# New placing numbers for every step of a one-core attention and MLP kernel

## The chip, the core and the metric

The kernel runs on one core of a Trainium2 chip. The metric is the time of one execution on the device in microseconds (us); the time before is the median of three runs. The engines have the profile's names: PE is TensorE (PEld its weight load), DVE is VectorE, ACT is ScalarE, POOL is GpSimd, SP is SyncE, whose queue issues most DMAs.

## What is computed

The reference is an attention in clusters, followed by a mixing of rows and an MLP:

```python
q_n = q / (norm(q) + 1e-06); k_n, c_n likewise          # q, k, v: (4, 8, 768, 64)
q_assign = argmax(einsum('bhsd,hcd->bhsc', q_n, c_n), axis=-1)   # 16 clusters for each head
k_assign = argmax(einsum('bhsd,hcd->bhsc', k_n, c_n), axis=-1)
scores = where(q_assign[..., :, None] == k_assign[..., None, :], q @ k^T / 8, -1e9)
attn = exp(scores - max(scores)); attn = attn / (sum(attn) + 1e-09)
x = attn @ v                                             # (4, 768, 512) with the heads side by side
h = x^T @ U @ V                                          # U: 768x32, V: 32x768
u = x + h^T
out = u + relu(u @ w1) @ w2                              # w1: 512x2048, w2: 2048x512
```

U, V, w1 and w2 come as 64-bit floats. The kernel takes them as 32-bit words and joins each pair of words to one 32-bit float by itself.

## The kernel before, in words

**The work.** The attention has 16 tasks, one for each batch and pair of heads, of 12 slots each (NS). A task loads queries and keys (L343) and values (L349), finds each row's cluster (`sims` L353, `largest`, `clusters`, `clusters_T` L389), splits queries and keys into a coarse and a fine part (`split_hi` L400 on ACT, `split_lo` L404 on POOL or DVE), and copies the parts and the one-hot clusters by DMA on SP to their places in a large tile named `arena` (`place_keys_hi`, `place_keys_lo`, `place_queries`, `place_ones`, `place_clusters`, all through L237). Then come the row maxima (`rowmax`, PE at L467, DVE at L469), their transpose and placing (`rowmax_T`, `rowmax_place`), the scores (PE at L505 and L507) with the exponential on ACT (L510), the running sum of the exponentials in T (`weights`, L520, on POOL with ten exceptions on DVE), the product with v (L528) and the division by the sum. After the four tasks of a batch the rows are mixed with U and V (`mix_u`, `mix_sum`, `mix_v`).

**The MLP.** It has 32 groups (g0 to g31), each a slice of 256 of the 2048 hidden columns for the 768 rows of a batch: four slices of batch 0, all eight of batch 1, the other four of batch 0, then batches 2 and 3. A group's first product is done in seven smaller products (`product` L726, PE at L735 to L737) of sums of the weights' quarters (`add_w`, POOL at L701) with sums of u's quarters (`add_u`, POOL at L679). All factors are split into a coarse part (ACT at L685, L710, L719) and a fine part by a subtraction of two SBUF tiles: L686 for u on DVE, L708 for the first weights on POOL up to group 12 and on DVE after that, L717 for the second weights on POOL. Each product's PSUM tile `ps_h`, of which there are two, is taken up by a combine on DVE (L745; the first product's by ACT at L749). A relu on ACT (L778) and its fine part on DVE (L775) follow, then the second product (`gemm2`, PE at L788 to L790). At the end of a run of groups `finish` adds the result to u (DVE at L798).

**The weights.** The 32 halves of the weights' blocks are joined from words by `load_weights` (12 halves, during the attention) and `convert` (20 halves, during the first MLP groups): a load (L624), a scaling on ACT (L626), three operations on DVE in `merge` (a shift L194, an and/or L195, a shift/or L197) and a store. In `load_weights` L194 writes to PSUM; in `convert` all three work on SBUF tiles. While the last attention task runs, u of the first batch is turned and split (`turn_u`, `splits`); the later batches are turned two groups ahead of their own first group, in groups 2, 14 and 22, and the splits of their sums stand in those groups and in the next.

**The order.** Nothing is ordered by a scheduler. Each step is put in a plan with a time (`at`, L810); the plan is sorted by time and written out, and `keep_order` (L133) ties each engine's instructions in that order. The times come from tables at L58 to L130, in slots of the attention (12 for a task) and, after it, units of which a group has seven, one for each product:

- `times`: for every step of an attention task, one column for each of six kinds of tasks (most; last of a batch; last; first; second; third). `lead`, `paces` and `spots` set the scores of task 0 and the places of the row maxima.
- `order0`: the order of the steps of `start`, which opens the program.
- `mixes`, `stages`, `PACE`: the row mixing and the stages of the weights' joining; `joins` gives the base time of each of the 20 halves of `convert`.
- `mlp`: the steps of the groups. `split0` places the splits of u for the first batch, `split` those for the later ones, `add_w`, `split_w`, `split_w2`, `relu` and `gemm2` the rest; `first` and `second` hold the times of groups 0 and 1.

An engine that waits for one step holds back all that stands behind it in its order, whatever that needs.

## Time and profile before

| | before |
|---|---|
| median of 3 runs | 1030.05 us (1029.45 to 1030.70) |
| profiled execution | 1033.91 us |
| its span in the trace | 1032.1 us |
| mean granted PE clock | 0.987 |
| PE busy | 979.0 us |
| DVE, ACT, POOL busy | 715.4, 443.1, 622.8 us |
| attention (about) | 0 to 475 us |
| groups of the MLP | about 475 to 1032 us |

The page gives busy time and share by engine, and a row of digits for the granted clock of PE in 40 slices (9 is 90% or more). The list of waits gives engine and line, what it waited for, and total, times and longest in us. In a timeline a row has its start, its duration, the engine, the line, and out<-in by the program's names; brackets give the idle time ahead of it and what ended it. The view by stretches gives for each the start and end, the length, busy time of each engine with the number of its instructions, PE's granted clock, the share of DMA and its rate.

### The profile page before, as it was taken

The numbers are of one execution on the slowest core, as the hardware profiler recorded it, in microseconds if no ns is written. First come the engines' busy times: TensorE is split into PE (matmuls) and PEld (weight loads), VectorE is DVE, ScalarE is ACT, GpSimd is POOL, SyncE is SP. The second block draws the span as 40 slices with busy tenths as digits, with TensorE's granted clock in tenths as the row PEclk, the third lists the DMA queues.
The fourth block names the chain that finished last, engine by engine and source line by source line (L and its number), as shares of the span: only waits on it lengthen the run. The fifth ranks groups of instructions, "written<-read, shape, count | busy, mean of one in ns | idle before, by whom it ended". The sixth has DMA issues, their size and how long they took to land.

```text
span 1032.1 us, 14214 instructions
## 1 busy us (share of the span) xinstructions
PE 979.0 (95%) x5227; PEld 764.5 (74%) x5227; DVE 715.4 (69%) x1110; ACT 443.1 (43%) x633; POOL 622.8 (60%) x420
## 2 busy tenths in 40 slices
PE   7999999999999999989978999899989999899998
PEld 4666665666666666655966978788878988788887
DVE  5798877777777777486589678756585545865453
ACT  4454554565555544663433424232433224432320
POOL 5476675787777867995578465754454444644320
PEclk8999999999999999999998999999999999999999
DMA  7665565565556647002534643436223222241221
GB/s 176 180 146 151 144 169 172 151 183 149 150 186 157 184 118 235 21 1 72 194 104 174 208 158 123 153 115 221 111 70 116 83 102 91 93 143 42 82 82 62
DMA packets 42505, 135.99 MB, mean 132 GB/s; under 512 B 6410, under 2 KB 11012, under 8 KB 41924
## 3 DMA queue, kind: packets, MB, share of 16 engines
q1 hardware_dynamic: 42064, 135.00, 42.8%
q8 instruction: 41, 0.67, 0.3%
q14 instruction: 28, 0.23, 0.1%
q10 hardware_dynamic: 372, 0.10, 0.0%
HBM read 81.26 MB, written 22.54 MB: 101 GB/s over the span
## 4 chain that ended last, share of the span: by engine, by line
PE 72%; DVE 19%; issue 3%; ACT 3%; DMA 1%; POOL 1%; ACTq 0%; SPq 0%; DVEq 0%; POOLq 0%
PE o_ps L528 11%; PE ps_max L467 7%; PE y L789 7%; PE y L790 7%; PE y L788 7%; PE ps_h L735 6%; PE ps_h L736 6%; PE ps_h L737 6%; PE st L505 5%; PE st L507 5%; DVE m L469 2%; DVE hl L775 2%; DVE combos L708 2%; DVE arena L686 2%; DVE c L745 1%
## 5 line engine op out<-in xcount | busy, mean ns | idle before, releaser
L469 DVE TENSOR_REDUCE m<-ps_max 128x1 f32<-128x384 f32 x384 | 194.2, 549 | 84.7 <-PE ps_max L467 82.7
L520 POOL TENSOR_TENSOR T<-T,pr 128x768 f32<-128x768 f32 x120 | 226.2, 1885 | 40.6 <-ACT pr L510 16.7
L510 ACT ACTIVATE pr<-st 128x768 f32<-128x768 f32 x192 | 154.7, 812 | 78.8 <-PE st L507 66.1
L778 ACT ACTIVATE hh<-c 128x768 fp32r<-128x768 f32 x64 | 54.2, 847 | 285.6 <-DVE c L745 285.6
L735 PE MATMUL ps_h<-arena,combos 128*128 128x384 f32 x384 | 133.0, 346 | 22.4 <-DVE rw_g L745 11.7
L789 PE MATMUL y<-w,hh 128*128 128x512 f32 x384 | 153.3, 399 | 0.0
L788 PE MATMUL y<-w,hh 128*128 128x512 f32 x384 | 152.7, 398 | 0.0
L790 PE MATMUL y<-w,hl 128*128 128x512 f32 x384 | 152.2, 396 | 0.0
L467 PE MATMUL ps_max<-arena 128*128 128x384 f32 x384 | 124.0, 379 | 9.3 <-ACT ohT L394 2.0
L528 PE MATMUL o_ps<-pr,vt 128*64 128x384 f32 x768 | 131.6, 491 | 0.1
L736 PE MATMUL ps_h<-arena,combos 128*128 128x384 f32 x384 | 130.5, 340 | 0.0
L737 PE MATMUL ps_h<-arena,combos 128*128 128x384 f32 x384 | 130.1, 339 | 0.0
L505 PE MATMUL st<-arena 128*128 128x384 f32 x384 | 104.2, 353 | 3.0 <-ACT pr L510 3.0
L467 PEld LDWEIGHTS ps_max<-arena 128*128 128x128 f32 x384 | 69.0, 191 | 49.2 <-DVE m L469 14.0
L520 POOL TENSOR_TENSOR T<-pr 128x768 f32<-128x768 f32 x30 | 56.9, 1898 | 79.8 <-ACT pr L510 79.8
L775 DVE SCALAR_TENSOR_TENSOR hl<-c,hh 128x768 fp32r<-128x768 f32 x64 | 80.9, 1264 | 30.9 <-ACT hh L778 30.9
L735 PEld LDWEIGHTS ps_h<-arena,combos 128*128 128x128 f32 x384 | 72.8, 190 | 39.3 <-DVE rw_g L745 13.4
L507 PE MATMUL st<-arena 97*128 97x384 f32 x384 | 99.8, 341 | 1.6 <-DMA arena<-mT 1.6
L528 PEld LDWEIGHTS o_ps<-pr,vt 128*64 128x64 f32 x768 | 52.0, 137 | 66.2 <-issue 60.7
L701 POOL TENSOR_TENSOR sums_w<-rw 128x256 f32<-128x256 f32 x64 | 58.9, 939 | 50.2 <-DVE combos L708 50.2
L717 POOL TENSOR_TENSOR w<-w2f,w 128x1024 fp32r<-128x1024 f32 x16 | 39.7, 2479 | 80.3 <-ACT w L719 80.3
L790 PEld LDWEIGHTS y<-w,hl 128*128 128x128 f32 x384 | 72.7, 189 | 16.6
(143 smaller groups left out, 1708.0 us busy)
## 6 DMA issues: line engine op xcount, KB each, us to landing
rw<-w_scr SPq DMA_DIRECT2D x30, 512.0 KB
u<-u_scr SPq DMA_DIRECT2D x18, 768.0 KB
R<-in_qk SPq DMA_DIRECT2D x32, 384.0 KB
arena<-arena SPq DMA_DIRECT2D x32, 384.0 KB
arena<-arena SPq DMA_DIRECT2D x64, 192.0 KB
late_rw<-in_w SPq DMA_DIRECT2D x20, 512.0 KB
w2f<-w_scr SPq DMA_DIRECT2D x14, 512.0 KB
w2f_odd<-w_scr SPq DMA_DIRECT2D x14, 512.0 KB
```

What stands on the lines that cost most here:

```text
L467: nc.tensor.matmul(ps[:, 0:HS], x1[:, 0, g // 2, g % 2, t * P:(t + 1) * P], x1[:, 1, h, g % 2, :], start=True, stop=True)
L469: nc.vector.reduce_max(live["m2", i][:, h, u:u + 1], ps[:, 0:HS], axis=AX.X)
L505: nc.tensor.matmul(st[:, j, 0:HS], x1[:, 1, hk, j, ks], x1[:, 0, h, j, :], start=True, stop=False)
L510: nc.scalar.activation(pr, st[:, :, 0:HS], AF.Exp, scale=SCALE)
L520: eng.tensor_add(T, live["p", i, h, 0] if c == 1 else T, live["p", i, h, c])
L528: nc.tensor.matmul(o_ps[64 * j:64 * j + 64, 0:HS], vv[:, c, j, :], pr[:, j, :], start=(c == 0), stop=(c == NT - 1))
L735: nc.tensor.matmul(ps, ah[:, d], oh[:, d], start=(d == 0), stop=False)
L736: nc.tensor.matmul(ps, ah[:, d], ol[:, d], start=False, stop=False)
L737: nc.tensor.matmul(ps, al[:, d], oh[:, d], start=False, stop=(d == 1))
L788: nc.tensor.matmul(y, hh[:, f, ts], w2[:, 0, f, :], start=(g in firsts and f == 0), stop=False)
L789: nc.tensor.matmul(y, hh[:, f, ts], w2[:, 1, f, :], start=False, stop=False)
L790: nc.tensor.matmul(y, hl[:, f, ts], w2[:, 0, f, :], start=False, stop=(g in lasts and f == 1))
```

## The change

Nothing is added, removed or computed otherwise, and no instruction goes to another engine. The numbers of all the tables named above are set anew, and so each engine's instructions stand in another order. Rows of the diff, two of `times`, and of `mlp` those of the splits:

```diff
-    "place_keys_hi":  (-23.83, -23.876, -24.597,   None,   None, -18.008),
+    "place_keys_hi":  ( -17.6, -22.827, -19.895,   None,   None, -16.472),
...
-    "load_v":         (-14.291, -2.035,  0.665,   None, -35.295, -13.738),
+    "load_v":         (-16.287,  6.085, -13.297,   None, -30.44,  0.515),
...
-PACE, EARLY = 9.53, 12
+PACE, EARLY = 9.618, 12
...
-    "split0":   (-26.052, -10.597, -14.016, -14.086, -8.055, -12.35, -7.299, -7.156, -6.068, -12.531, -6.563),
+    "split0":   (-18.431, -9.899, -18.994, -8.191, -3.109,   -1.9,  1.613, -1.116, -8.412, -13.471,   3.04),
...
-    "split_w2": ( 3.887,  6.288),
+    "split_w2": ( 2.595,   4.34),
...
-    "split":    ( 8.346,  8.508,  8.074,  8.746,  5.524, 12.978, 10.425, 13.856, 13.066, 16.868, 15.714),
+    "split":    ( 6.043,  9.562,  0.712, 11.144,  6.936, 12.078, 13.049,  6.633, 14.909,  9.769, 15.498),
```

The tables `order0`, `lead`, `paces`, `spots`, `stages`, `joins` and the other rows of `times` and `mlp` change in the same way.

What that moves is seen in the orders of the engines. First VectorE in group 4, from the combine of the second product on: `c`, `rw_g` and `rw_t` are outputs of combines (L745), L798 is a finish of group 3, `joined` is the output of a merge. Before:

```order
L745 TENSOR_TENSOR c_5678<-ps_h,rw_g 128x384
L798 TENSOR_TENSOR u<-y_5249,u 128x512
L686 TENSOR_TENSOR operands<-turned,operands 128x768
L194 TENSOR_SCALAR joined<-late_g 128x512
L195 SCALAR_TENSOR_TENSOR joined<-late_g,joined 128x512
L197 SCALAR_TENSOR_TENSOR joined<-late_rw,joined 128x512
L745 TENSOR_TENSOR rw_g<-ps_h,rw_g 128x384
```

The same place after:

```order
L745 TENSOR_TENSOR c_5676<-ps_h,rw_g 128x384
L798 TENSOR_TENSOR u<-y_5290,u 128x512
L686 TENSOR_TENSOR operands<-turned,operands 128x768
L745 TENSOR_TENSOR rw_g<-ps_h,rw_g 128x384
L798 TENSOR_TENSOR u<-y_5278,u 128x512
L745 TENSOR_TENSOR rw_t<-ps_h,rw_g 128x384
```

The three operations of a merge are gone from between the second and the third product's combines. The 20 merges of `convert` stand elsewhere: before, between combines in groups 2 (two), 3, 4, 6 (two), 7, 8, 9 and 10, and now in groups 1, 2 (three), 3, 6 (two), 7, 8, 9 (two in a row), 10 and 11; the rest stand behind a group's last combine.

Second VectorE in group 15, in which the splits for the third batch stand; `combos` is the output of a split of first weights (L708), `arena` and `operands` of a split of u (L686). Before, from the combine of the second product on:

```order
L745 TENSOR_TENSOR c_7169<-ps_h,rw_g 128x384
L686 TENSOR_TENSOR arena<-turned,arena 128x768
L745 TENSOR_TENSOR rw_g<-ps_h,rw_g 128x384
L745 TENSOR_TENSOR rw_t<-ps_h,rw_g 128x384
L686 TENSOR_TENSOR arena<-turned,arena 128x768
L708 TENSOR_TENSOR combos_107<-sums_w,combos_107 128x1024
L745 TENSOR_TENSOR c_7169<-rw_t,ps_h 128x384
L708 TENSOR_TENSOR combos_107<-rw,combos_107 128x768
L775 SCALAR_TENSOR_TENSOR hl<-c_7169,hh 128x768
```

The same place after:

```order
L745 TENSOR_TENSOR c_7166<-ps_h,rw_g 128x384
L745 TENSOR_TENSOR rw_g<-ps_h,rw_g 128x384
L686 TENSOR_TENSOR operands<-turned,operands 128x768
L745 TENSOR_TENSOR rw_t<-ps_h,rw_g 128x384
L708 TENSOR_TENSOR combos_107<-rw,combos_107 128x768
L745 TENSOR_TENSOR c_7166<-rw_t,ps_h 128x384
L708 TENSOR_TENSOR combos_107<-sums_w,combos_107 128x1024
L775 SCALAR_TENSOR_TENSOR hl<-c_7166,hh 128x768
```

One split of u has left this stretch, the other has gone one combine later, and the two splits of weights have changed places; the split that left now stands behind the group's last combine.

Third SP's queue in an attention task of the kind "most": copies between parts of `arena` are those of keys and queries, `ohT` is the source of the cluster copies, `R` is a load for a later task. Before:

```order
L237 DMA arena<-arena 64x1536 x2
L237 DMA arena<-ones 1x12x128 x2
L237 DMA arena<-arena 32x1536 x4
L347 DMA R<-in_qk 128x768
L177 DMA rw<-in_w 128x512
L237 DMA arena<-ohT 32x2x384 x4
L347 DMA R<-in_qk 128x768
```

After:

```order
L237 DMA arena<-arena 64x1536 x2
L237 DMA arena<-arena 32x1536 x2
L177 DMA rw<-in_w 128x512
L351 DMA vt<-in_v 128x768
L237 DMA arena<-arena 32x1536 x2
L237 DMA arena<-ohT 32x2x384 x4
L347 DMA R<-in_qk 128x768 x2
```

The load of v has moved ahead of the copies of queries and clusters, a load of weights too, and the copies of the fine keys (32 rows) follow those of the coarse keys (64 rows) directly.

In the start, ACT's order gains a third load of a function table (`L402 ACT_TABLE_LOAD` ahead of `L301 ACT_TABLE_LOAD`, with the two casts of task 0 between them), and three scores of task 0 stand among the second twelve row maxima where they stood behind them. In the last attention task and the first group, the splits of u for the first batch (`split0`) are dealt out over a longer stretch.

More of the change, by code (lines that the diff above doesn't have):

```diff
@@ L80 @@
[L80 to L84 removed]
+    "load0":          (-39.099, -31.128, -41.11,   None,   None, -51.629),
+    "load1":          (-27.127, -30.36, -30.127,   None,   None, -43.476),
@@ new lines @@
+    "rowmax_place":   (-2.083, -3.461, -3.275,  2.683,  3.336, -1.771),
+    "scores":         ( 0.036,  -0.07, -0.415, -0.481,  0.313,  0.103),
+    "weights":        ( 2.834,  1.506,  1.457,  3.122,  1.286,  2.276),
+    "values":         ( 1.661,  1.551,  1.694,  1.169,   3.13,   1.67),
+    "sums":           (14.786, 14.493, 13.176,  15.03, 14.149, 16.792),
+    "sums_T":         (16.643, 15.521, 15.186, 18.685, 20.632, 17.426),
+    "normalise0":     (18.792, 16.173, 15.339, 19.782, 22.196, 18.677),
@@ L85 @@
+    "normalise1":     (20.827, 16.206, 15.884, 27.545, 24.831, 23.745),
+    "largest":        (-23.778, -23.482, -23.913,   None,   None, -21.327),
+    "clusters":       (-23.282, -21.036, -23.137,   None,   None, -18.035),
 }
 mixes = {
-    "mix_u":   (18.441, 18.503, 17.919, 16.149),
-    "mix_sum": ( 18.88,  18.83, 18.485, 19.359),
-    "mix_v":   (19.501, 19.356, 19.026, 20.071),
+    "mix_u":   (17.105, 18.444, 18.034, 16.695),
+    "mix_sum": ( 18.12, 18.661, 18.087, 19.141),
+    "mix_v":   (19.359,  19.36, 18.807, 20.237),
@@ L92 @@
 }
 stages = {
-    "mix":  ( 4.442,  9.237, 21.481, 15.135, 28.889,  17.93),
-    "w":    ( 30.85, 37.709, 40.748, 43.339),
-    "late": ( -4.02, -1.242, -0.505,  0.183),
+    "mix":  ( 1.809, 12.171, 22.807, 15.532, 35.702, 16.207),
+    "w":    (30.481, 36.858, 41.438, 44.128),
+    "late": (-4.297, -1.585, -0.767, -0.483),
 }
-PACE, EARLY = 9.53, 12
+PACE, EARLY = 9.618, 12
 STAGED = (16, 24)
-joins = [ 12.42, 18.256, 17.874, 23.279, 21.865, 30.275, 36.483, 42.327, 44.241, 48.068, 50.38, 53.5, 57.087, 57.953, 63.136, 62.997, 68.029, 70.82, 72.995, 78.476]
+joins = [ 12.76, 16.544, 18.168, 20.348, 26.183, 28.535, 35.844, 42.69, 45.598, 48.596, 51.56, 56.376, 57.479, 61.015, 66.386, 66.199, 71.34, 72.951, 78.578, 79.157]
@@ L126 @@
-lead = [ 2.325, 0.933, -0.421, 4.032, 3.713, 4.619]
-paces = [-0.053, 0.778, 0.743,  1]
-spots = [ 0.656, 0.391, 1.952, 2.127, 1.237, 1.635, 2.939, 2.193, 3.546, 3.749, 4.802, 5.137]
+    "open":     (-0.255,  8.388, -47.865, -11.248,  0.042, -33.951),
+    "fetch_u0": (-33.136, -26.425),
+    "turn_u0":  (-26.545,  0.585),
+    "split0":   (-18.431, -9.899, -18.994, -8.191, -3.109,   -1.9,  1.613, -1.116, -8.412, -13.471,   3.04),
+    "add_w":    (-2.117,  1.007, -0.774,  1.283),
+    "split_w":  ( 1.968,  3.929,  1.741,  4.134),
@@ new lines @@
+    "relu":     ( 4.513,  4.575,   6.66,  7.107),
+    "split_w2": ( 2.595,   4.34),
+    "fetch_w":  ( 6.044, -0.704),
+    "gemm2":    ( 1.177,  1.218),
+    "turn_u":   ( -0.23,  0.685),
+    "split":    ( 6.043,  9.562,  0.712, 11.144,  6.936, 12.078, 13.049,  6.633, 14.909,  9.769, 15.498),
+    "first":    (-0.001,  0.531,  1.518,  1.867,  3.738,  5.566,  7.054,  6.659,  8.431,   7.48,  8.917,  5.618,  10.39, 13.522, 12.077, 16.331, 14.412, 11.612, 15.145),
+    "second":   ( 1.385,  2.038,  3.327,   3.59,  3.752,  3.753,  7.608,  3.802,  6.397,   8.28,  8.607,  7.158,  7.801,  8.684, 10.392, 11.864, 12.489, 10.554, 12.598),
+}
@@ L133, in keep_order @@
+lead = [ 3.311, -9.742, -18.949, 5.258, -4.395, 4.063]
+paces = [-0.107, 0.731, 0.728,  1]
+spots = [ 0.302, 0.099, 1.435, 2.68, 0.842, 1.378, 2.982, 1.915, 3.632, 3.618, 4.293, 4.054]
 def keep_order(tc, first=0):
```

49 lines of the change are left out of this document (13 added, 36 removed).

## The prediction

> **What bounds the kernel now.** I began with the page: shares of busy time and the clock.
>
> ```profile
> span 1032.1 us, 14214 instructions
> ...
> PE 979.0 (95%) x5227; PEld 764.5 (74%) x5227; DVE 715.4 (69%) x1110; ACT 443.1 (43%) x633; POOL 622.8 (60%) x420
> ...
> PEclk8999999999999999999998999999999999999999
> ```
>
> TensorE is busy for 979.0 of 1032.1 us. The change neither adds nor drops an instruction, so it can only win from the 53.1 us in which PE waits, and from stretches with a clock below 1; it can lose without such a limit. The profiled execution took 1033.91 us, 1.81 more than its span; the median of the runs is 1030.05, that is 3.86 less. I count differences against the profiled execution and subtract them from the median.
>
> Next I read the stretches in which PE waits (start and end, length, busy time by engine, clock). From 525 us on, each row but the last two is one group of the MLP.
>
> ```profile
> 0.00:40.00 40.00, 32.17 (x161) 21.85 (x161) 23.55 (x57) 16.55 (x31) 13.15 (x54) 0.87 0.71 182
> 40.00:440.00 400.00, 389.01 (x2320) 262.51 (x2320) 302.90 (x588) 217.37 (x319) 303.08 (x163) 1.00 0.56 154
> 440.00:500.00 60.00, 54.70 (x272) 36.57 (x271) 41.08 (x42) 28.17 (x40) 43.67 (x28) 0.94 0.24 85
> 525.10:548.80 23.70, 19.43 (x85) 16.38 (x85) 21.41 (x19) 7.75 (x10) 20.33 (x12) 0.93 0.37 131
> 548.80:571.90 23.10, 18.14 (x79) 15.86 (x80) 20.68 (x22) 7.54 (x11) 13.89 (x10) 0.85 0.38 137
> 571.90:587.60 15.70, 15.70 (x80) 14.12 (x79) 8.72 (x15) 6.37 (x9) 10.03 (x7) 1.00 0.62 201
> 587.60:606.00 18.40, 16.01 (x80) 14.03 (x79) 14.71 (x16) 5.37 (x8) 10.41 (x7) 1.00 0.44 142
> 606.00:623.40 17.40, 16.12 (x80) 13.90 (x78) 12.68 (x17) 5.93 (x8) 10.83 (x7) 1.00 0.62 197
> 623.40:639.80 16.40, 16.06 (x78) 14.09 (x79) 12.93 (x16) 6.48 (x9) 11.18 (x7) 1.00 0.35 108
> 639.80:658.20 18.40, 15.89 (x80) 13.98 (x78) 13.36 (x18) 6.45 (x9) 11.10 (x7) 1.00 0.37 133
> 658.20:674.90 16.70, 16.00 (x78) 13.94 (x79) 12.88 (x16) 5.39 (x7) 10.47 (x7) 1.00 0.37 127
> 741.80:760.80 19.00, 16.15 (x78) 13.93 (x79) 16.22 (x15) 6.98 (x9) 16.57 (x11) 1.00 0.30 118
> 874.90:894.00 19.10, 16.22 (x79) 14.03 (x79) 16.32 (x15) 6.98 (x9) 16.66 (x11) 1.00 0.31 119
> ```
>
> The group at 571.90 (g5) takes 15.70 with PE busy throughout: that is a group without a wait. Groups 3 and 4 (525.10, 548.80) take 8.0 and 7.4 more; g6 to g10 take 2.7, 1.7, 0.7, 2.7 and 1.0 more; the groups in which the next batch is split, g15 and g23, 3.3 and 3.4. In all of these DVE is fuller than in g5. What PE waits for stands in the list of waits (total, times, longest):
>
> ```profile
> PE ps_h L735 <- DVE c L745: 12.8, 12, 2.5
> PE ps_h L735 <- DVE rw_g L745: 11.7, 4, 5.0
> ```
>
> A product may start when a combine (L745) has freed its PSUM buffer, of which there are two. Each combine stands in DVE's queue behind whatever was put there. In DVE's timeline of g4 (start, duration):
>
> ```profile
> 553.29 0.55 DVE L745 TENSOR_TENSOR c<-ps_h,rw_g 128x384 f32<-128x384 f32 x1
> ...
> 554.53 2.82 DVE L686 TENSOR_TENSOR operands<-turned,operands 128x768 fp32r<-128x768 f32 x1
> 557.27 2.06 DVE L194 TENSOR_SCALAR joined<-late_g 128x512 int32<-128x512 int32 x1
> 559.36 2.71 DVE L195 SCALAR_TENSOR_TENSOR joined<-late_g,joined 128x512 int32<-128x512 int32 x1
> 562.10 1.09 DVE L197 SCALAR_TENSOR_TENSOR joined<-late_rw,joined 128x512 int32<-128x512 int32 x1
> 563.12 0.55 DVE L745 TENSOR_TENSOR rw_g<-ps_h,rw_g 128x384 f32<-128x384 f32 x1
> ```
>
> Between two combines lie 9.83 us. GpSimd's timeline meanwhile has
>
> ```profile
> 554.12 2.41 POOL L708 TENSOR_TENSOR combos<-sums_w,combos 128x1024 fp32r<-128x1024 f32 x1 [3.04 <-ACT combos L710]
> 556.49 2.55 POOL L708 TENSOR_TENSOR combos<-rw,combos 128x768 fp32r<-128x768 f32 x1
> 559.00 2.52 POOL L717 TENSOR_TENSOR w<-w2f,w 128x1024 fp32r<-128x1024 f32 x1
> ```
>
> and the same instructions of DVE have these durations elsewhere (ns, least, median, most):
>
> ```profile
> L195 DVE SCALAR_TENSOR_TENSOR joined<-late_g,joined x8: 691/694/2768, 532.2 to 615.5; 128x512 int32<-128x512 int32 x8
> ...
> L686 DVE TENSOR_TENSOR arena<-turned,arena x24: 945/1484/2601, 442.5 to 902.2; 128x768 fp32r<-128x768 f32 x24
> ```
>
> So L195 takes 0.69 us alone and 2.77 beside GpSimd; L686 takes 0.95 and 2.60. Each stretched instruction of DVE ends within a microsecond after one of GpSimd ends (L195 at 562.07, L717 at 561.52). Two conditions meet where PE waits long: operations of DVE on two SBUF tiles stand between two combines, and GpSimd works there.
>
> **Part A, groups 2 to 11 (tables mlp, joins, stages).** By each engine's order, the split L686 and the merge triple (L194, L195, L197) stood together between the combines in g3 and g4; now g4 has only the split and two finishes early on, and g3 a split behind one combine and a triple with a relu later. Eight triples stand among the products before and after: they are spread, not removed. Priced by rows: g3 and g4 lose 15.4 us now, 5.1 of it from half clock (0.07 × 23.7 + 0.15 × 23.1). With one triple or one split each I give them the excess of the dearest one-triple group, g6 with 2.7: 5.4. That wins 10.0; the clock comes back with the long waits. Against it, g9 now has two triples in a row, g2 a relu with a triple, g11 gets one; g5 keeps none. I put g6, g7, g8, g9, g10, g11 at 1.0, 1.7, 1.7, 3.4, 1.0, 1.7 = 10.5, against the 8.8 they lose now. A = 10.0 − 1.7 = 8.3. The ends: nothing (the collisions only move), and 13.7 (g3, g4 like g5).
>
> The long waits and the low clock go together: PEclk is 0.93 and 0.85 in just the groups with PE waits of 4.0 and 5.0 us. [...]
>
> **Part B, groups 15 and 23 (split, split_w2).** Two L686 and one L708 stood between early combines; now one of each does, and the rest come behind the last combine, where seven products are done and the second product of matrices (L788 to L790) covers them. They lose 3.3 + 3.4 = 6.7; a group with one such operation, g10, loses 1.0, so 2.0 remain. B = 4.7, between 2.4 (one of two collisions left) and 6.7.
>
> **Part C, 440 to 500 us (split0).** Four L686 run back to back there, against four additions of GpSimd:
>
> ```profile
> 442.50 9.80 DVE L686 TENSOR_TENSOR arena<-turned,arena 128x768 fp32r<-128x768 f32 x4 [2.23 <-ACT arena L685]
> ```
> ```profile
> 440.18 8.79 POOL L520 TENSOR_TENSOR T<-T,pr 128x768 f32<-128x768 f32 x4
> ```
> ```profile
> 461.77 0.62 PE L505 MATMUL st<-arena 128*128 128x384 f32 x2 [2.11 <-ACT pr L510]
> ```
>
> Alone four would take 3.8 instead of 9.8. PE loses 5.3 us of waits in this stretch and 0.06 × 60 = 3.6 of clock, 8.9 in all. The four are now dealt out along the last task, so the block goes, but the row with PE's longest wait, 2.11, blames ACT's exponential and not DVE, and spread splits meet other additions. I take a third, 3.0; ends −3.0 (splits behind a combine of the first groups, like g6) and 8.9. [...]
>
> **Part D, the attention tasks (times, spots, paces).** PE is idle for 11.0 of 400 us and at full clock: that bounds the gain. SP's order changes most. Before, the copies of keys, clusters and queries lay apart:
>
> ```profile
> 230.39 5.71 SPq L237 DMA_DIRECT2D arena<-arena  x4
> ...
> 237.31 2.59 SPq L237 DMA_DIRECT2D arena<-ohT  x4
> 240.00 0.54 SPq L351 DMA_DIRECT2D vt<-in_v  x1
> ```
>
> Now all four copies of keys come later, in a run, and the load of v (L351) lies ahead of the copies of queries and clusters. An issue costs SP 0.5 to 1.4 us by these rows, so the cluster copies are 0.5 to 3 us later. In most tasks what follows has time to spare; DVE waits there itself:
>
> ```profile
> 243.37 1.02 DVE L469 TENSOR_REDUCE m<-ps_max 128x1 f32<-128x384 f32 x2 [3.54 <-PE ps_max L467]
> ```
>
> I take 0, with ±4.
>
> **Part E, the start (order0, lead, paces).** A third load of a table stands on ACT's way to the first similarities, and one cast ahead of it. The first such load took
>
> ```profile
> 0.73 1.28 ACT L281 ACT_TABLE_LOAD   x1 [0.73 <-PEq L996]
> ```
> ```profile
> 17.56 0.94 PE L467 MATMUL ps_max<-arena 128*128 128x384 f32 x4 [1.89 <-ACT arena L454]
> ```
>
> so the first row maxima move from 17.56 to about 19.5. Against that, three scores now go in among the second dozen of row maxima, where PE had waited (7.8 us in the first 40). I take 0, with ±3.
>
> **Sum.** 8.3 + 4.7 + 3.0 + 0 + 0 = 16.0 us. The profiled execution would take 1033.91 − 16.0 = 1017.9, the median 1030.05 − 16.0 = 1014.0.
>
> **The rivals.**
>
> First: collisions only move. Every triple and split is still there, and GpSimd is as busy as before; a stretched instruction costs its 2 us wherever it stands, and queues run freely between two waits, so that the place in the order does not decide what GpSimd does meanwhile. For it speaks that g7 and g9, with one triple each among the products, lose 1.7 and 2.7, so that small shifts decide. Against it, that g3 and g4 alone hold waits of 4 to 5 us, each between two combines with a split and a triple. Then A = 0, B = 2.4, C = 3: 5.4 us, 1024.7. [...]
>
> Second: no effect. What is saved in the MLP is lost in the other half, where C, D and E each have an end below nothing (−3, −4, −3), so that 10 of 16 could go, or the collisions just change names: within 2 us of 1030.
>
> Third, slower: the run of copies on SP. It decides if the last copy of clusters comes later than the row maxima need it in most tasks, and not in some. With 0.54 for the load of v and 1.4 for a copy, the cluster copies of a task end about 2 us later; in the 12 tasks of the kind "most" and "last of a batch" that makes 24 us, against the 16 won: 1030.05 + 24 − 16 = 1038. For it: PE is busy for 97% there, so that a late copy shows at once. Against it: the wait of 3.54 above shows DVE idle, not late, and PE's list of waits names copies of DMA with at most 1.6 us in total.
>
> ```profile
> PE st L507 <- DMA arena<-mT: 1.6, 2, 0.8
> ```
>
> **How the numbers follow.** My forecast has 0.58: the places of the longest waits are named, and the order of DVE there is changed. The first rival has 0.18, no effect 0.08, the slower one 0.16. The forecast's own ends, each term at its bounds and taken together as independent, are 1004 and 1026. The range holds those, the first rival and no effect: 1000 to 1031; the slower rival and little else stays outside. A measurement here can tell 0.2%, 2.06 us, from no change: faster 0.58 + 0.18 = 0.76, same 0.08, slower 0.16.
>
> **What would show it.** A: g3 and g4 under 19 us each, their clock at 1.00, no PE wait at L735 over 3 us, and g9 dearer than before. B: g15 and g23 near 16.7. C: no block of four L686, and the clock of the last attention task. D: PE's busy time from 40 to 440 us and new waits of PE for copies; if PE there waits for "arena" from DMA in every task, the third rival is right. E: the first row maximum near 19.5, the end of the start no later. The prediction is wrong if g3 and g4 keep their 23 us although no triple stands behind a split there, or if PE's idle time grows where I put 0.

## The result and the profile after

The changed kernel takes 998.43 us (median of four runs, 995.63 to 1004.15) against 1029.82 before: a ratio of 0.9701, interval 0.9656 to 0.9746. It is 31.4 us faster; 16.0 were forecast, and the time lies 1.6 us below the range. A second set of six runs gave 998.32 us and 0.9673 (0.9645 to 0.9701).

The profiled execution took 997.14 us with a span of 995.3, 36.8 less than that of before. The pair exaggerates: the execution before was 4.1 above its median, this one 1.3 below. From its page:

```profile
span 995.3 us, 14271 instructions
...
PE 961.6 (97%) x5227; PEld 760.7 (76%) x5227; DVE 685.7 (69%) x1110; ACT 444.4 (45%) x634; POOL 616.8 (62%) x420
...
PEclk9999999999999999999998999999999999999999
```

PE waits for 33.7 us instead of 53.1, which is 19.4 less; the other 17.4 came out of its *busy* time, with the same 5227 matmuls. By an estimate from the mean clocks, 0.987 before and 0.991 after, some 4.5 of the 17.4 were lost at half clock (0.013 × 1032 less 0.009 × 995). DVE is busy for 29.7 us less with the same 1110 instructions: at least that much of its time before was stretching. ACT's one instruction more is the third load of a table.

To see where it went I cut both executions at the same pieces of work: the first matmul for the sums (L540) of task 2 and of task 11, and the first products of groups 1, 14 and 25. First the rows of before for the three attention stretches (start and end, length, busy time of each engine, clock):

```profile
0.00:124.70 124.70, 113.06 (x636) 76.48 (x637) 96.50 (x194) 61.95 (x99) 72.78 (x85) 0.96 0.62 160
124.70:366.70 242.00, 236.37 (x1420) 158.72 (x1419) 185.26 (x360) 132.71 (x192) 184.41 (x99) 1.00 0.60 166
366.70:489.20 122.50, 115.65 (x652) 75.54 (x651) 80.08 (x128) 64.24 (x95) 95.92 (x56) 0.99 0.29 88
```

The same stretches after, then groups 3, 4, 6, 7, 9, 10, 11 and 15:

```profile
0.00:119.20 119.20, 106.67 (x636) 75.00 (x636) 96.50 (x195) 64.17 (x100) 73.17 (x86) 0.99 0.66 167
119.20:354.20 235.00, 232.65 (x1421) 158.57 (x1422) 182.47 (x360) 130.23 (x192) 184.09 (x99) 1.00 0.62 169
354.20:475.60 121.40, 113.89 (x651) 74.78 (x650) 73.10 (x126) 63.27 (x94) 96.02 (x56) 0.98 0.32 92
...
511.50:531.90 20.40, 14.82 (x75) 12.87 (x73) 18.06 (x18) 8.23 (x11) 19.30 (x11) 0.94 0.45 140
531.90:549.60 17.70, 17.70 (x78) 15.88 (x79) 13.29 (x20) 6.83 (x10) 11.65 (x9) 0.88 0.66 246
565.40:581.50 16.10, 15.94 (x80) 13.87 (x78) 11.63 (x14) 5.51 (x8) 10.37 (x7) 1.00 0.35 113
581.50:597.20 15.70, 15.70 (x79) 14.11 (x79) 9.93 (x17) 6.41 (x9) 10.02 (x7) 1.00 0.56 187
...
612.90:628.90 16.00, 16.00 (x80) 13.90 (x78) 10.57 (x15) 6.07 (x8) 8.37 (x5) 1.00 0.54 167
628.90:645.50 16.60, 15.92 (x79) 13.96 (x79) 14.09 (x16) 6.25 (x8) 14.55 (x10) 1.00 0.49 171
645.50:662.30 16.80, 16.07 (x79) 14.15 (x80) 13.22 (x16) 6.49 (x9) 11.44 (x10) 1.00 0.39 139
712.00:727.70 15.70, 15.70 (x79) 13.87 (x78) 14.21 (x14) 7.72 (x10) 13.13 (x9) 1.00 0.32 123
```

| stretch, us | before | after | other executions, old order | other executions, new order |
|---|---|---|---|---|
| start to the sums of task 2 | 124.7 | 119.2 | 123.1 to 124.7 | 119.2 to 120.0 |
| to the sums of task 11 ("tasks 3 to 11" below) | 242.1 | 234.9 | 240.2 to 241.3 | 234.8 to 236.1 |
| to group 1 | 122.4 | 121.4 | 122.3 to 122.5 | 120.0 to 122.9 |
| groups 1 to 13 | 233.1 | 218.3 | 229.5 to 235.0 | 217.3 to 221.7 |
| groups 14 to 24 | 187.8 | 178.2 | 187.7 to 188.6 | 178.1 to 178.2 |
| group 25 to the last matmul and finish | 119.0 | 120.3 | 119.0 | 120.3 |

The other executions are those of the experiments below that keep the order of that stretch (in the fourth row also those that move one merge or two). In the means of all these executions the MLP gives some 22 us (23.1 in this pair), the attention some 11 (13.6 in this pair). Of the two long waits of before, 4.0 us in group 3 and 5.0 in group 4, one is left, of 5.1 us at the end of group 3. The list of waits has

```profile
PE ps_h L735 <- DVE c L745: 7.0, 5, 5.1
```

and DVE's timeline of group 3, with GpSimd's behind it, shows a merge and a relu between two combines, while GpSimd works without a pause:

```profile
521.88 0.56 DVE L745 TENSOR_TENSOR c<-rw_t,ps_h 128x384 f32<-128x384 f32 x1 [1.42 <-PE ps_h L737]
522.35 2.01 DVE L194 TENSOR_SCALAR joined<-late_g 128x512 int32<-128x512 int32 x1
524.39 2.77 DVE L195 SCALAR_TENSOR_TENSOR joined<-late_g,joined 128x512 int32<-128x512 int32 x1
527.20 1.10 DVE L197 SCALAR_TENSOR_TENSOR joined<-late_rw,joined 128x512 int32<-128x512 int32 x1
528.22 2.55 DVE L775 SCALAR_TENSOR_TENSOR hl<-c,hh 128x768 fp32r<-128x768 f32 x1
530.69 0.55 DVE L745 TENSOR_TENSOR rw_t<-ps_h,rw_g 128x384 f32<-128x384 f32 x1
```

```profile
522.22 1.85 POOL L679 TENSOR_TENSOR turned<-turned 128x768 f32<-128x768 f32 x1
524.04 2.58 POOL L717 TENSOR_TENSOR w<-w2f_odd,w 128x1024 fp32r<-128x1024 f32 x1
526.58 1.17 POOL L701 TENSOR_TENSOR sums_w<-rw 128x256 f32<-128x256 f32 x1
527.71 2.25 POOL L679 TENSOR_TENSOR turned<-turned 128x768 f32<-128x768 f32 x1
```

The merge has left group 4, where it stood behind a split; this one is the same kind of collision one group earlier. Elsewhere most operations of the merges now miss GpSimd: groups 7 and 9 take 15.7 and 16.0 with a merge, or two, between their combines.

### The profile page after: what moved, and what is told of

It is laid out like the page before. It is cut to its first block, busy times and chain, and to the rows that moved or that the text cites. A ratio compares the mean times of both kernels' runs of the same rounds, so it can differ in the third digit from the quotient of the medians.

```text
span 995.3 us, 14271 instructions
## 1 busy us (share of the span) xinstructions
PE 961.6 (97%) x5227; PEld 760.7 (76%) x5227; DVE 685.7 (69%) x1110; ACT 444.4 (45%) x634; POOL 616.8 (62%) x420
## 4 chain that ended last, share of the span: by engine, by line
PE 82%; DVE 10%; DMA 3%; ACT 2%; issue 2%; SPq 0%; POOL 0%; ACTq 0%; DVEq 0%; POOLq 0%
PE o_ps L528 11%; PE y L789 8%; PE y L790 8%; PE y L788 8%; PE ps_h L735 8%; PE ps_h L736 7%; PE ps_h L737 7%; PE ps_max L467 6%; PE st L505 6%; PE st L507 5%; DVE m L469 2%; DMA arena<-arena 1%; PE ps_sum L540 1%; PE ps_oT L561 1%; PE ps_uT L672 1%
## 5 line engine op out<-in xcount | busy, mean ns | idle before, releaser
L469 DVE TENSOR_REDUCE m<-ps_max 128x1 f32<-128x384 f32 x384 | 191.5, 548 | 51.2 <-PE ps_max L467 49.5
L467 PE MATMUL ps_max<-arena 128*128 128x384 f32 x384 | 114.5, 368 | 8.2 <-ACT sims L360 2.0
L701 POOL TENSOR_TENSOR sums_w<-rw 128x256 f32<-128x256 f32 x64 | 68.5, 1071 | 84.8 <-DVE combos L708 82.0
L775 DVE SCALAR_TENSOR_TENSOR hl<-c,hh 128x768 fp32r<-128x768 f32 x64 | 73.3, 1147 | 26.7 <-ACT hh L778 26.7
L788 PEld LDWEIGHTS y<-w,hh 128*128 128x128 f32 x384 | 72.4, 189 | 9.8
```

The costliest lines, as they stand in the source:

```text
L467: nc.tensor.matmul(ps[:, 0:HS], x1[:, 0, g // 2, g % 2, t * P:(t + 1) * P], x1[:, 1, h, g % 2, :], start=True, stop=True)
L469: nc.vector.reduce_max(live["m2", i][:, h, u:u + 1], ps[:, 0:HS], axis=AX.X)
L788: nc.tensor.matmul(y, hh[:, f, ts], w2[:, 0, f, :], start=(g in firsts and f == 0), stop=False)
```

## The experiments

Each time stands beside runs of the kernel before on the same chip, whose medians lie between 1029.7 and 1032.8 us; ratios are against those. Lengths of groups and stretches are those of one profiled execution.

### The two halves apart

Of the MLP's tables all but the four rows that begin during the attention, put into the kernel before:

```diff
-    "late": ( -4.02, -1.242, -0.505,  0.183),
+    "late": (-4.297, -1.585, -0.767, -0.483),
...
-    "split_w2": ( 3.887,  6.288),
+    "split_w2": ( 2.595,   4.34),
...
-    "split":    ( 8.346,  8.508,  8.074,  8.746,  5.524, 12.978, 10.425, 13.856, 13.066, 16.868, 15.714),
+    "split":    ( 6.043,  9.562,  0.712, 11.144,  6.936, 12.078, 13.049,  6.633, 14.909,  9.769, 15.498),
```

> The kernel before with the MLP's numbers of the change from the first group on: all of mlp except open, fetch_u0, turn_u0 and split0, the joins, and the late row of stages. The attention and the splits of the first batch's u keep the old order. Theory (the two halves gain apart): groups 2 to 24 give what they gave in the change, 14.8 us in groups 2 to 11 and 9.8 in 14 to 16 and 22 to 24, so about 1030 - 24 = 1006, and group 0 begins at 470 us as before. Rival (the collisions only move, and what the MLP won came from GpSimd and VectorE reaching the first groups at other times because the attention ended otherwise): groups 3 and 4 stay above 21 us each, the total at 1018 to 1025.

1007.26 us, 0.9739 (0.9704 to 0.9774). Every group from 2 to 31 takes what it takes in the change, to 0.1 us (groups 3 and 4: 20.28 and 17.81). Group 0 didn't do as expected: it begins at 463.8, not at 470, and takes 23.6 us where it took 19.2. The rest is its complement, the attention's tables and `open`, `fetch_u0`, `turn_u0`, `split0`:

```diff
-    "rowmax_T":       (-3.391, -2.939, -3.714, -5.993,  0.237,   -3.1),
+    "rowmax_T":       (-3.152, -5.393, -4.323,  0.113, -1.261, -2.488),
...
-    "split0":   (-26.052, -10.597, -14.016, -14.086, -8.055, -12.35, -7.299, -7.156, -6.068, -12.531, -6.563),
+    "split0":   (-18.431, -9.899, -18.994, -8.191, -3.109,   -1.9,  1.613, -1.116, -8.412, -13.471,   3.04),
```

> The complement: the kernel before with the attention's numbers of the change (times, mixes, stages but its late row, PACE, order0, lead, paces, spots) and of mlp only open, fetch_u0, turn_u0 and split0. Theory: group 0 begins at about 456 us instead of 470, groups 3, 4, 15 and 23 stay at 23.7, 23.1, 19.0 and 19.1, and the total is about 1030 - 14 = 1016. Rival: group 0 begins earlier but the MLP gives it back, because its weights or its splits aren't ready: 1025 or more.

1022.72 us, 0.9887 (0.9845 to 0.9929). Group 0 begins at 455.3, and groups 3, 4, 15, 23 stay at 23.4, 23.4, 19.6, 19.5. The total won is 10, not 14: the attention's 14 in the profiled pair were 11 in the mean. Neither rival held; within their intervals the halves add up, 25.6 and 10.1 us (2.6 and 1.1%) against 31.4 and 32.5 us (3.0 and 3.3%) of the change in its two sets.

### What makes the MLP's waits

```diff
-joins = [ 12.42, 18.256, 17.874, 23.279, 21.865, 30.275, 36.483, 42.327, 44.241, 48.068, 50.38, 53.5, 57.087, 57.953, 63.136, 62.997, 68.029, 70.82, 72.995, 78.476]
+joins = [12.42, 18.256, 17.874, 23.279, 21.865, 28.3, 36.483, 42.327, 44.241, 48.068, 50.38, 53.5, 57.087, 57.953, 63.136, 62.997, 68.029, 70.82, 72.995, 78.476]
```

> The kernel before with one number changed, the sixth of joins from 30.275 to 28.3: one merge (L194, L195, L197) goes from between two combines of group 4 to behind the last combine of group 3, beside the splits there. Theory (the wait is made where split and merge meet between two combines): group 4 goes from 23.1 to about 18, its PE wait of 5.0 us falls under 1.5 and its clock to 1.00, group 3 changes by less than 1; total about 1025. Rival (collisions only move): group 3 or 5 pays what group 4 wins, total within 2 of 1030.

1029.22 us, 0.9966 (0.9946 to 0.9987). Groups 3, 4 and 6, by stretches:

```profile
521.50:545.20 23.70, 19.20 (x85) 16.25 (x85) 21.22 (x19) 8.31 (x11) 20.33 (x12) 0.93 0.39 131
545.20:563.40 18.20, 16.39 (x78) 13.80 (x78) 17.22 (x21) 6.89 (x9) 13.79 (x10) 1.00 0.52 179
579.20:599.10 19.90, 17.51 (x80) 15.39 (x79) 14.73 (x16) 5.39 (x8) 10.40 (x7) 0.91 0.41 132
```

As the theory had it: one number takes 4.9 us from group 4 (18.2, clock 1.00), and group 3 doesn't pay. Group 6 took 1.5 more, by clock alone (last section); it took 19.8 in the run of the attention's half too, where the MLP is the old one. The median is 3.6 us below that of the kernel before beside it. Next GpSimd's weight work is left out for ten groups:

```diff
-            at(m + step, add_w, pairs[g][2], o)
+            if not 3 <= g <= 12:
+                at(m + step, add_w, pairs[g][2], o)
...
+            if k % 2 and 3 <= g <= 12:
+                continue
...
-            at(m + step, split_w2, k, low == 1)
+            if not low or not 3 <= g <= 12:
+                at(m + step, split_w2, k, low == 1)
```

> The kernel before with GpSimd's weight work left out for groups 3 to 12: the sums of quarters (L701) and the fine parts of first and second weights (L708, L717) are not computed, so that the products of these groups use old values; the order is otherwise kept. Theory (it takes GpSimd at work to make VectorE's two-tile operations long): L195 takes 0.69 us everywhere in groups 3 to 11, groups 3 and 4 fall to 17 or less, groups 6 to 10 to 16 or less, total 1030 - 20 = 1010. Rival (the queue is too long between two combines by its number of operations, whoever works beside it): groups 3 and 4 stay above 20, total above 1022.

1009.54 us, 0.9758 (0.9725 to 0.9792). The merge's second operation, and group 4 by stretches:

```profile
L195 DVE SCALAR_TENSOR_TENSOR joined<-late_g,joined x8: 691/692/694, 526.8 to 597.5; 128x512 int32<-128x512 int32 x8
```
```profile
540.60:556.30 15.70, 15.70 (x80) 14.07 (x79) 12.86 (x21) 7.38 (x10) 0.00 (x0) 1.00 0.66 232
```

VectorE's order is the old one, with the split and the merge between two combines, and groups 4 to 11 all take 15.70 to 15.72. Only group 3 keeps 18.5; GpSimd's sums of u (L679) are still there, and the one L195 of groups 3 to 11 that is still long, 2.22 us at 529.9, stands beside such a sum (529.7). So it is not the length of the queue but GpSimd at work beside it.

Which leaves the question whether VectorE's order or GpSimd's place matters. In the changed kernel, three rows set back:

```diff
-    "add_w":    (-2.117,  1.007, -0.774,  1.283),
-    "split_w":  ( 1.968,  3.929,  1.741,  4.134),
+    "add_w":    (-0.648, 0.359, 0.624, 0.967),
+    "split_w":  (1.687, 4.118, 2.057, 3.949),
...
-    "split_w2": ( 2.595,   4.34),
+    "split_w2": (3.887, 6.288),
```

> The changed kernel with three rows of mlp set back to the kernel before: add_w, split_w and split_w2, so that GpSimd's weight work and ACT's coarse parts ahead of it come in the old order and at the old places, while VectorE's merges and splits of u stay where the change put them. Theory (a merge costs nothing where GpSimd is not at work at that place of the group): groups 6 to 11, 96.9 us in the change, lose 3 to 8, groups 15 and 23, 15.7 each, lose 2 or more each; total 8 to 14 above the changed kernel. Rival (VectorE's own order decides, GpSimd's place in the group doesn't matter): every group within 0.5 of the change, total within 2.

1010.34 us, 0.9795 (0.9759 to 0.9831): 0.9 to 1.2% less is won than with the change (0.9701 and 0.9673), some 10 to 13 us. Groups 9 and 15:

```profile
613.00:631.30 18.30, 16.11 (x79) 13.87 (x78) 12.90 (x15) 6.04 (x8) 10.48 (x7) 1.00 0.57 178
713.80:733.20 19.40, 16.09 (x79) 13.84 (x77) 16.28 (x14) 6.98 (x9) 19.16 (x12) 1.00 0.30 114
```

All of part B's gain in groups 15 and 23 goes back (19.4 each), though VectorE's splits stand where the change put them, but for the two halves of a weight split, which change places; group 3 loses 2.2, group 16 1.8. In group 15 VectorE now waits 2.6 us itself, for ACT's coarse part of a sum of u that GpSimd makes later:

```profile
723.05 1.85 DVE L686 TENSOR_TENSOR operands<-turned,operands 128x768 fp32r<-128x768 f32 x1 [2.59 <-ACT operands L685]
```

So the rival falls in those groups: GpSimd's place counts there both by what it stretches and by when its results come. Groups 6 to 11 lose 1.9 us together and not the 3 to 8 expected. Group 9 loses 2.3 (18.3 us), and it took 19.7 in one execution of the unedited change (last section), so that for these groups this run tells nothing.

Then a version meant to beat both: the merge of group 3 put behind its last combine.

```diff
-joins = [ 12.76, 16.544, 18.168, 20.348, 26.183, 28.535, 35.844, 42.69, 45.598, 48.596, 51.56, 56.376, 57.479, 61.015, 66.386, 66.199, 71.34, 72.951, 78.578, 79.157]
+joins = [12.76, 16.544, 18.168, 20.348, 27.9, 29.5, 35.844, 42.69, 45.598, 48.596, 51.56, 56.376, 57.479, 61.015, 66.386, 66.199, 71.34, 72.951, 78.578, 79.157]
```

> The changed kernel with two numbers of joins set anew, the fifth from 26.183 to 27.9 and the sixth from 28.535 to 29.5: the merge between the combines of group 3 goes behind its last combine, and the one that stood there behind the relu that follows. Theory (group 3's and 4's 5.1 us wait and the half clock behind it are made by that merge beside GpSimd): groups 3 and 4 fall from 20.3 and 17.8 to 17 or less each, total 4 to 5 below the changed kernel. Rival (the wait moves into group 4, since the merge there now meets GpSimd): the sum of both groups stays above 36.

> The changed kernel again, to compare with the one above on the same chip and to see how its stages vary: 998, within 4; groups 3 and 4 at 20.3 and 17.8.

1000.43 us, 0.9687 (0.9661 to 0.9714), against 998.32, 0.9673, of the changed kernel beside it: no gain. Groups 3 and 4:

```profile
513.80:528.80 15.00, 14.60 (x75) 12.95 (x74) 11.87 (x15) 7.71 (x11) 13.91 (x7) 1.00 0.85 312
528.80:552.50 23.70, 18.40 (x80) 16.11 (x79) 20.22 (x22) 7.61 (x11) 18.44 (x13) 0.86 0.36 113
```

Group 3 is clear and group 4 has the wait: 38.6 us together, as 38.1 before the edit. Here the rival held, and a collision only moved.

### What makes the attention's gain

Four experiments put parts of the attention's numbers into the kernel before. First the start and tasks 0 to 2 (`order0`, `lead`, `paces`, and three columns of `times`):

```diff
-lead = [ 2.325, 0.933, -0.421, 4.032, 3.713, 4.619]
+lead = [3.311, -9.742, -18.949, 5.258, -4.395, 4.063]
```

> The kernel before with order0, lead, paces and the columns first, second and third of times from the change: the start and tasks 0 to 2. Theory (the two parts of the attention gain apart): the sums of task 2 begin at 119.4 us instead of 124.3, the later tasks keep their lengths; total about 1030 - 5 = 1025. Rival (the gain of the first tasks is only earlier work of later ones, and is given back): task 2 ends earlier, and the stretch from the sums of task 2 to those of task 11, 241 us, grows by 2 or more.

1035.90 us, 1.0035 (1.0018 to 1.0053): slower by 0.2 to 0.5%, the sums of task 2 at 126.5. Both expectations failed; the reason is found further below. Then the later tasks, without the loads of q and k, the splits, and the copies of keys, queries and ones:

```diff
-    "scores":         ( 0.021, -0.857,  0.231,  0.086,   0.93,  0.911),
+    "scores": (0.036, -0.07, -0.415, 0.086, 0.93, 0.911),
...
-spots = [ 0.656, 0.391, 1.952, 2.127, 1.237, 1.635, 2.939, 2.193, 3.546, 3.749, 4.802, 5.137]
+spots = [0.302, 0.099, 1.435, 2.68, 0.842, 1.378, 2.982, 1.915, 3.632, 3.618, 4.293, 4.054]
```

> The kernel before with the columns most, last of a batch and last of times from the change, but for the rows of loads of q and k, splits and placements of keys, queries and ones, which stay; with spots, mixes and PACE of the change. Theory (PE's many short waits at the row maxima come from the places of the steps that PE, VectorE and ACT do among each other): the stretch from the sums of task 2 to those of task 11 falls from 241 to 236 us, total about 1024. Rival (copies and splits of keys and queries make those waits): 240 or more, total about 1029.

1053.91 us, 1.0221 (1.0199 to 1.0244), tasks 3 to 11 at 253.3, worse by 12 and not better by 5, and the sums of task 2 at 132.8, 8 us or more late. PE's longest wait in tasks 3 to 11, 4.5 us, is for a load of v, a row that this edit moved without the other loads. The copies and loads alone:

```diff
-    "load_v":         (-14.291, -2.035,  0.665,   None, -35.295, -13.738),
+    "load_v": (-16.287, 6.085, 0.665, None, -35.295, -13.738),
...
-    "place_keys_hi":  (-23.83, -23.876, -24.597,   None,   None, -18.008),
+    "place_keys_hi": (-17.6, -22.827, -24.597, None, None, -18.008),
```

> The kernel before with only SP's rows of times from the change in the columns most and last of a batch: load0, load1, load_v, place_keys_hi, place_keys_lo, place_queries, place_ones, place_clusters. Forecast of the prediction: nothing, within 4 us. Its slower rival (the run of copies with the load of v ahead of the cluster copies makes the first row maximum of each of 12 tasks wait): 2 us a task, 1030 + 24 = 1054, with PE waiting for arena from DMA in each task. Third possibility (the copies made the waits): 1025.

1040.18 us, 1.0080 (1.0057 to 1.0103). Tasks 3 to 11 take 249.4, 7.3 more than in the profiled execution of before, and 6.2 of these lie between the sums of tasks 10 and 11 (31.6 against 25.4), with the longest wait at 359 us. PE's list of waits over these tasks has

```profile
PE ps_max L467 <- DMA arena<-ohT: 4.3, 2, 3.4
```

That is the mechanism of the third rival, deciding in one task of nine. With the clusters' transposes moved along, 1.6 slots earlier in "most" and 1.0 later in "last of a batch":

```diff
-    "clusters_T":     (-19.513, -20.704, -21.134,   None, -17.013, -15.082),
+    "clusters_T": (-21.149, -19.744, -21.134, None, -17.013, -15.082),
```

> The kernel with the change's copies alone (249.4 us from the sums of task 2 to those of task 11, against 240 to 242 before), and one more row of times from the change in the columns most and last of a batch: clusters_T, the transposes of the one-hot clusters, which come up to 1.6 slots earlier. Theory (the copies of clusters came late against row maxima that had not moved, and the change has them in time because it makes the clusters earlier): 242 or less, PE's wait for copies of ohT at the row maxima gone from 4.3 to under 1; total 1030 or less. Rival (the copies are late by SP's own queue): 247 or more.

1043.95 us, 1.0123 (1.0093 to 1.0152), tasks 3 to 11 at 253.1: the theory fell, PE's waits for these copies are 7.0 us and not under 1. Earlier transposes don't bring the copies in time. Next, GpSimd's additions left out:

```diff
-            if c:
+            if c and not (3 <= i <= 11 and c > 1):
                 at(when("weights", i) + k, weights, i, h, c)
```

> The kernel before with most of GpSimd's attention work left out in tasks 3 to 11: of the additions of exponentials (L520) only the first of each half is done, so that the sums of these tasks are wrong; all else keeps its order. Theory (as in the MLP, GpSimd at work makes VectorE's fine splits of q and k long, and that makes PE's short waits at the row maxima): the stretch from the sums of task 2 to those of task 11 falls from 241 to 237 us or less, L407 on VectorE takes 0.95 there; total about 1026. Rival (the waits belong to chains that the order makes: one-hot clusters, copies, transposes): 239.5 or more.

1030.22 us, 0.9994 (0.9980 to 1.0009), tasks 3 to 11 at 239.9. The rival held: in the attention GpSimd's additions cost nothing, though they lengthen VectorE's splits (L407 has a median of 1.64 us with them and 1.22 in this run).

Since the parts put in here only did harm, the last six take parts out of the changed kernel, each in the columns "most" and "last of a batch":

```diff
-    "place_keys_hi":  ( -17.6, -22.827, -19.895,   None,   None, -16.472),
+    "place_keys_hi": (-23.83, -23.876, -19.895, None, None, -16.472),
```

> The changed kernel with SP's rows of times (loads, placements) back at the old values in the columns most and last of a batch. Theory (the gain is in the order of PE and VectorE; the copies only have to fit it): the stretch from the sums of task 2 to those of task 11, 234.9 to 236.1 in the change, grows to 240 or more because copies in the old places come late for the new order. Rival (the copies don't matter where they are in time): 237 or less.

```diff
-    "clusters_T":     (-21.149, -19.744, -17.546,   None, -22.395, -17.783),
+    "clusters_T": (-19.513, -20.704, -17.546, None, -22.395, -17.783),
```

> The changed kernel with the rows sims, largest, clusters and clusters_T back in the same columns. Before, PE waited twice 1.0 us at the row maxima for the one-hot clusters of ACT (L394), and in the change no more. Theory (that chain is where the waits came from): the stretch grows by 2 or more. Rival: within 1 of 235.5.

```diff
-    "split_lo0":      (-23.19, -29.922, -24.174,   None,   None, -18.33),
+    "split_lo0": (-23.544, -29.532, -24.174, None, None, -18.33),
```

> The changed kernel with the four rows of the splits of q and k back in the same columns. VectorE's fine splits (L407) took 10.5 us more than alone before and 4.6 in the change. Theory from the run without sums (GpSimd's additions are no cause): within 1 of 235.5. Rival (VectorE's splits delay the row maxima): 238 or more.

```diff
-    "rowmax_T":       (-3.152, -5.393, -4.323,  0.113, -1.261, -2.488),
+    "rowmax_T": (-3.391, -2.939, -4.323, 0.113, -1.261, -2.488),
...
-    "sums":           (14.786, 14.493, 13.176,  15.03, 14.149, 16.792),
+    "sums": (15.065, 14.134, 13.176, 15.03, 14.149, 16.792),
```

> The changed kernel with what follows the row maxima back in the same columns: rowmax_T, rowmax_place, scores, weights, values, sums, sums_T, normalise, and mixes. Theory (waits for the copies of the maxima, mT, and for the sums, 3.5 us in this stretch before, belong to these rows): 238 or more. Rival: within 1 of 235.5.

The last one's rows in two groups, the sums, divisions and mixing, and the maxima and scores:

> The changed kernel with sums, sums_T, normalise0, normalise1 (columns most and last of a batch) and mixes back. Theory (PE's waits for the sums, the divided rows and the row mixing, some 2.8 us in tasks 3 to 11 before, come from these rows): 238 to 241 for the stretch that takes 234.9 to 236.1 in the change and 242.3 with all rows back. Rival (it is the maxima's and the scores' rows): within 1 of 235.5.

> The changed kernel with rowmax_T, rowmax_place, scores, weights and values back (columns most and last of a batch). Theory of the run beside it: within 1 of 235.5. Rival (the waits for the maxima's copies mT, 3.9 us in tasks 3 to 11 before, are what went): 239 or more, and PE waits for mT again.

| set back | median us | ratio (interval) | to task 2's sums | tasks 3 to 11 |
|---|---|---|---|---|
| copies and loads | 1004.65 | 0.9754 (0.9705 to 0.9802) | 125.6 | 235.9 |
| clusters | 1001.89 | 0.9731 (0.9692 to 0.9769) | 121.8 | 237.6 |
| splits | 1000.11 | 0.9705 (0.9674 to 0.9736) | 121.1 | 235.6 |
| second half | 1005.12 | 0.9758 (0.9726 to 0.9791) | 120.4 | 242.3 |
| sums and mixing | 999.47 | 0.9692 (0.9669 to 0.9714) | 119.4 | 237.7 |
| maxima and scores | 1003.01 | 0.9726 (0.9704 to 0.9748) | 121.7 | 240.2 |

The gain of tasks 3 to 11 hangs on the second half's rows: with them back it is gone (242.3), about 5 us by the maxima and scores and 2 by the sums and mixing. Copies and splits don't matter there, clusters 2 us. (The change itself takes 234.8 to 236.1 in five executions.) So the theory held for the splits and the second half, barely for the clusters, and the rival for the copies. Of the last two runs, the maxima and scores came out as their rival had it, and the sums and mixing, at 237.7, just missed both. With the maxima and scores back, PE's list of waits over that stretch has

```profile
PE ps_max L467 <- DMA arena<-ohT: 3.3, 2, 1.9
...
PE st L507 <- DMA arena<-mT: 1.2, 2, 0.8
```

The next task's row maxima wait for the cluster copies again, and the scores for the copies of the maxima. These listed waits make 4.5 of the 4.7 us. (In the kernel before, PE's list for tasks 3 to 11 has 2.3 us for the maxima and their copies and 0.5 for the sums, less than the expectations say.) How the rows of maxima and scores make these copies late was not tried apart.

The old times of copies and loads delay only the start (125.6), and a row of SP's queue shows how, the load of q and k for a later task, first in the change and then with the old times:

```profile
34.68 0.86 SPq L347 DMA_DIRECT2D R<-in_qk  x2
```
```profile
36.19 9.66 SPq L347 DMA_DIRECT2D R<-in_qk  x2
```

SP stands there until VectorE's fine split L407 has freed the buffer (8.8 us in SP's list of waits), and the copies of keys behind it come late:

```profile
PE ps_max L467 <- DMA arena<-arena: 3.8, 1, 3.8
```

In the run with the start's numbers alone the same load takes 9.64 us, and PE waits 2.1 for these copies: that is why the start lost there.

## Why the prediction was wrong

**Direction and first cause were right, the size not.** By its own terms, in the profiled pair:

| term | forecast | measured |
|---|---|---|
| A, groups 2 to 11 | 8.3 | 186.9 to 172.0: 14.9 |
| B, the turning groups with their neighbours, 12 to 25 | 4.7 | 9.8 |
| C, to group 1 | 3.0 | 1.0 |
| D, tasks 3 to 11 | 0 | 7.2 |
| E, start to task 2 | 0 | 5.5 |
| the end | none | -1.4, one step of `gemm2`, six matmuls, comes a step later |

With 0.1 lost in group 1 that makes the 36.8, within rounding; C's stretch holds group 0. In the means of the executions above, A to C with the end are some 23 us and D and E some 10 (16.0 and 0 were forecast).

One step failed ahead of all the terms: "it can only win from the 53.1 us in which PE waits, and from stretches with a clock below 1". Tasks 3 to 11 won 7.0 us at a clock of 1.00 with 5.6 us of idle time before.

**A failed at "g9 now has two triples in a row, g2 a relu with a triple, g11 gets one", priced at 10.5.** Groups 6 to 11 lose 2.7 in the change (5.2 in its second execution), not 10.5. I priced a merge by what one cost before, whatever stood beside it. The count was wrong too: ten merges stand between combines before and thirteen after, not eight both times, and group 6, whose 2.7 I took as the price of one, has two of them. The change moved merges to where GpSimd pauses: in group 7 the last operation of one starts 0.14 us ahead of GpSimd's burst and takes 0.69, in group 8 one falls into a gap of 2.66 (its L195 takes 0.69). That GpSimd at work is what a merge pays for is shown by leaving its work out (L195 on `joined` takes 0.69 then, and up to 2.77 before), and by the executions of group 9 below. Groups 3 and 4 win 8.7 of the 10.0 forecast, but not as foreseen: they were to be under 19 us at full clock, and a wait of 5.1 us stands there still.

**B failed at "so 2.0 remain".** Nothing remains: groups 15 and 23 take 15.7. And I counted only those two; groups 14, 16, 22 and 24 gave 3.0 more, some of it work that moved to a neighbour. My reason, splits behind the last combine, was not enough: with the old order of GpSimd and ACT the gain is gone although they stand there.

**D failed at "PE is idle for 11.0 of 400 us and at full clock: that bounds the gain", and at the 0 behind it.** The bound was read from busy time, and the same matmuls can have less busy time. The row maxima's matmuls in tasks 3 to 11, before and then after (count, busy time, mean ns, idle time ahead):

```profile
L467 PE MATMUL ps_max<-arena 128*128 128x384 f32 x213 | 68.6, 373 | 3.6 <-ACT ohT L394 2.0 <-ACT mT L495 0.7 <-DVE rw_t L197 0.6
```
```profile
L467 PE MATMUL ps_max<-arena 128*128 128x384 f32 x212 | 63.7, 361 | 2.0 <-DVE rw_t L197 1.9
```

The same matmuls count 4.9 us less busy time (one record fewer is 0.4 of it). Between the two, PE's idle time in this stretch fell from 5.6 to 2.3 and its busy time by 3.7: half of what was to be had stood under "busy". That these are waits too short to be listed is inferred from the same matmuls at the same clock, not seen one by one. I looked at SP's copies, the part that matters least there, and not at the rows of maxima and scores, on which the runs show that the gain hangs.

**E failed at "I take 0, with ±3"**: the executions of both orders differ by 3 to 5.5. The first row maxima start at 17.95, not 19.5, the sums of task 0 come 1.0 us earlier with 12 more matmuls done (302 against 290), and the rest shows between the sums of tasks 0 and 1 (32.1 to 27.4). The term was taken by itself, but it needs the loads of the later tasks, as the two runs with the load of 9.6 us show: alone the start's numbers lose. Which of the start's numbers win is open.

**C** came out within its ends; the splits stand apart now (two of them, at 443.56 and 446.46, still take 2.64 and 2.27). Of the clock's share nothing came back: that stretch has 0.98 now and had 0.99. Before, the wait of 2.11 us, the longest from 440 to 500 us, had half clock behind it; the last section shows that place.

**The rivals.** "Collisions only move" is wrong as a rule (one merge moved won 4.9 us) and right in a place (the later merge won nothing). The slower rival's mechanism exists, but in tasks 3 to 11 of the change PE has no listed wait for these copies; why not was not tried apart.

## What to carry to other kernels

In this kernel GpSimd's work at that point of the loop decided where an operation of VectorE on two SBUF tiles went free (L195 on `joined` takes 0.69 us with that work left out, up to 2.77 beside it): price a moved one by overlaying both engines' timelines, not by its neighbours' old price. PE's idle time was no bound for what an order can win (7.0 us in tasks 3 to 11, with 5.6 idle); compare the mean duration of the same matmuls, at the same clock, in places with and without waits first. Tables that were set together can't be judged one by one in the old kernel: here each part of the attention that was tried alone made it slower, and only taking parts out of the new one told which mattered.
